# An attention and FFN kernel: FFN chunks that run on over the batches, and the last token tiles stored in four DMAs each

## Chip, cores, metric

The kernel runs on one core of one Trainium2 chip (trn2). The metric is the device time of one execution in microseconds. Beside the times there is one profiled execution of every kernel; its span runs from the first to the last recorded instruction and is about 2 us shorter than the device time. Executions come in two states. In the slower one the start-up takes 2 to 4 us longer; only fast runs are compared below, and times within one trace are counted from the end of the start-up where that matters.

## The reference

Linear attention with a quadratic feature map feeds a two-layer FFN with squared ReLU. The cut reference:

```python
# q, k, v: (4, 4, 1088, 32); S1, S2: (8, 32); w_in: (128, 2048); w_out: (2048, 128)
phi(x) = outer(S1 @ x, S2 @ x)                # 64 features a head
kv  = sum over tokens of phi(k) v ;  z = sum of phi(k)
attn = (phi(q) kv) / (phi(q) z + 1e-6)
x = attn, as 4352 tokens of 4 heads * 32 = 128 features
h = maximum(x @ w_in, 0)
out = (h * h) @ w_out                         # (4352, 128), float32
```

The FFN is most of the work: 4352 columns (tokens) times 16 blocks of 128 hidden features.

## The kernel before

All tokens stand as columns of `xT` (128 features on the partitions). A chunk of n columns runs through 16 blocks. A block is one matmul with w_in (fp32r), a ReLU on ScalarE, a square on ScalarE or VectorE, and one product with w_out in fp32, which appears in the trace as two instructions. By the paces that the prediction reads at three sizes (0.686, 0.820 and 0.953 us at 320, 384 and 448 columns), a block costs 2.083 ns a column and 20 ns beside. In the same trace (before) the starts of its two w_out instructions lie 269, 322 and 375 ns apart, 0.83 ns a column more, which is two fifths of the 2.083. From that I estimate two fifths for each of the two and one fifth, 0.417 ns a column, for the w_in matmul. TensorE's order is static: the w_out product of unit u, then the w_in matmul of unit u + 4. (A unit is one block, or mostly two where a block has 256 columns.) The attention of the next batch is cut into pieces (`kc`, `kvp`, `qc`, `nd`) that are put between the blocks. The chunk lists restart at every batch, so a batch of 1088 tokens has three chunks, 12 in all:

```python
FC = [[(0, 256), (256, 384), (640, 448)]] + [[(0, 384), (384, 384), (768, 320)]] * (B - 2)
FC += [[(0, 448), (448, 384), (832, 256)]]
...
def ffn1(u, i):                                  # w_in
    nc.tensor.matmul(st["pg", u][:, n * i : n * i + n],
                     w_in[:, 128 * (d0 + i) : 128 * (d0 + i) + 128],
                     st[b, "xT"][:, c0 : c0 + n])
...
def ffn2(u, i, xs=None):                         # w_out, the ordinary chunks
    nc.tensor.matmul(po[0][:, 0:n], w, g, start=(d == 0), stop=(d == NB - 1))
```

The last chunk (256 tokens) is token-major: the w_out weights stream and the result is two tiles of 128 tokens x 128 features, `obl`. Each goes out in one DMA, one from ScalarE, one from SyncE:

```python
def store(eng, i):
    eng.dma_start(
        bass.AP(out.tensor, out.offset + (b * S + c0 // 32 + 4 * i) * 128,
                [[128, 4], [G * 128, 32], [1, 128]]),
        ob[i][:, :])

nc.scalar.copy(ob[0][:, :], po[0][:, 0:128])
store(nc.scalar, 0)
nc.vector.tensor_copy(ob[1][:, :], po[1][:, 0:128])
store(nc.sync, 1)
```

## Time and profile before

| | before |
|---|---|
| device time, median of the first runs | 188.1 us |
| span of the profiled run | 186.1 us |
| TensorE busy | 180.4 us (97%) |
| last matmul ends, after the start of the span | 182.21 us |
| end of the last copy to the end of the span | 3.51 us |

The prediction shows the lines that carry the bound. Two groups of the page's costliest instructions are added here:

```profile
L619 PE MATMUL po<-g,w_o 128*128 128x384 f32 (+3 forms) x352 | 138.4, 478 | 0.0
L581 PE MATMUL pg<-xT,w_in 128*128 128x384 f32 (+3 forms) x192 | 110.2, 582 | 0.5 <-ACT gt L590 0.5
```

```profile
L1069 ACTq DRAIN  x2: 8/246/485, 182.3 to 185.6; - x2
```

The last column of the groups says that TensorE hardly ever stood idle before an FFN matmul (0.5 us in all): whatever is gained there must come from the matmuls' own pace.

### The profile page before, as it was taken

The numbers are of one execution on the slowest core, as the hardware profiler recorded it, in microseconds if no ns is written. First come the engines' busy times: TensorE is split into PE (matmuls) and PEld (weight loads), VectorE is DVE, ScalarE is ACT, GpSimd is POOL, SyncE is SP. The second block draws the span as 40 slices with busy tenths as digits, with TensorE's granted clock in tenths as the row PEclk, the third lists the DMA queues.
The fourth block names the chain that finished last, engine by engine and source line by source line (L and its number), as shares of the span: only waits on it lengthen the run. The fifth ranks groups of instructions, "written<-read, shape, count | busy, mean of one in ns | idle before, by whom it ended". The sixth has DMA issues, their size and how long they took to land.

```text
span 186.1 us, 4132 instructions
## 1 busy us (share of the span) xinstructions
PE 180.4 (97%) x1561; PEld 120.8 (65%) x1562; DVE 116.7 (63%) x263; ACT 149.3 (80%) x329; POOL 35.8 (19%) x157
## 2 busy tenths in 40 slices
PE   8998999999999999999999999999999999999991
PEld 2766766666555566666577666656577655666891
DVE  4979989958991699379934689379943412222400
ACT  3509778878979889789698989789698998999960
POOL 2736405327400000184000000185000000000000
PEclk9999999999999999999999999999999999999999
DMA  5899600100039600200059200200020200020200
GB/s 181 201 301 330 168 0 5 28 4 0 4 48 250 153 4 0 45 3 0 13 120 270 38 4 0 42 4 0 8 40 0 35 0 2 8 41 4 30 12 28
DMA packets 24555, 11.27 MB, mean 61 GB/s; under 512 B 17880, under 2 KB 23000, under 8 KB 24536
## 3 DMA queue, kind: packets, MB, share of 16 engines
q1 hardware_dynamic: 24084, 10.82, 24.5%
q8 instruction: 12, 0.20, 0.5%
q10 hardware_dynamic: 452, 0.20, 0.4%
q14 instruction: 7, 0.06, 0.1%
HBM read 8.78 MB, written 2.23 MB: 59 GB/s over the span
## 4 chain that ended last, share of the span: by engine, by line
PE 95%; DMA 2%; DVE 1%; ACT 0%; issue 0%; POOL 0%; ACTq 0%; DVEq 0%
PE po L619 60%; PE pg L581 18%; PE nd L531 3%; PE kvp L397 2%; PE pol L614 2%; PE po L614 2%; PE qc L299 2%; DMA s_nat<-in_S_dram 2%; PE kvp L379 1%; PE kf L309 1%; PE kc L299 1%; PE x L713 1%; ACT gt L590 0%; PE den L774 0%; PE num L774 0%
## 5 line engine op out<-in xcount | busy, mean ns | idle before, releaser
L619 PE MATMUL po<-g,w_o 128*128 128x384 f32 (+3 forms) x352 | 138.4, 478 | 0.0
L581 PE MATMUL pg<-xT,w_in 128*128 128x384 f32 (+3 forms) x192 | 110.2, 582 | 0.5 <-ACT gt L590 0.5
L590 ACT ACTIVATE gt<-pg 128x384 f32<-128x384 f32 (+4 forms) x177 | 85.3, 489 | 19.3 <-PE pg L581 16.1
L619 PEld LDWEIGHTS po<-g,w_o 128*128 128x128 f32 x352 | 62.5, 189 | 22.6 <-issue 7.4
L598 ACT ACTIVATE g<-gt 128x384 f32<-128x384 f32 (+3 forms) x138 | 70.9, 531 | 2.9
L581 PEld LDWEIGHTS pg<-xT,w_in 128*128 128x128 f32 x192 | 36.0, 189 | 25.0 <-issue 6.0
L600 DVE TENSOR_TENSOR g<-gt 128x384 f32<-128x384 f32 (+4 forms) x39 | 21.9, 563 | 38.4 <-ACT gt L590 38.4
L438 POOL COPY kv<-kvt 32x64 f32<-32x64 f32 x48 | 11.8, 246 | 71.3 <-PE po L619 63.0
L492 POOL COPY rd<-rc 32x9 f32<-32x9 f32 (+2 forms) x80 | 16.6, 207 | 13.2 <-DVE rc L484 9.9
L501 DVE STREAM_SHUFFLE qa<-qc 128x576 f32<-128x576 f32 (+2 forms) x20 | 11.6, 648 | 0.0
L516 DVE TENSOR_TENSOR qp<-qa,qb 128x576 f32<-128x576 f32 (+2 forms) x20 | 10.8, 600 | 0.0
L464 DVE STREAM_TRANSPOSE qt<-qc 128x576 f32<-128x576 f32 (+2 forms) x10 | 5.8, 615 | 6.2 <-PE qc L299 6.2
L350 DVE TENSOR_TENSOR kp<-fs 128x576 f32<-128x576 f32 x12 | 8.2, 741 | 0.0
L623 DVE STREAM_TRANSPOSE oT<-po 128x384 f32<-128x384 f32 (+3 forms) x11 | 6.1, 559 | 1.8 <-PE po L619 1.8
L531 PE MATMUL nd<-qp,kv 32*32 32x288 f32 (+2 forms) x320 | 6.8, 353 | 0.0
L341 DVE STREAM_TRANSPOSE fs<-kc 128x576 f32<-128x576 f32 x6 | 4.3, 762 | 3.2 <-PE kc L299 3.2
L550 DVE TENSOR_TENSOR xT<-nd,bc 128x576 fp32r<-128x576 f32 (+2 forms) x10 | 5.6, 600 | 1.0 <-PE nd L531 1.0
L531 PEld LDWEIGHTS nd<-qp,kv 32*32 32x32 f32 x320 | 3.8, 103 | 3.6 <-issue 1.7
L501 DVE STREAM_SHUFFLE qb<-qc 128x576 f32<-128x576 f32 (+2 forms) x10 | 6.0, 646 | 0.0
L541 DVE STREAM_TRANSPOSE bc<-rd 128x576 f32<-128x576 f32 (+2 forms) x10 | 5.8, 606 | 0.2
L292 DVE STREAM_TRANSPOSE qT<-qn 128x192 f32<-128x192 f32 (+3 forms) x11 | 5.8, 564 | 0.0
L614 PE MATMUL pol<-w_o,g 128*128 128x128 f32 x32 | 5.7, 275 | 0.0
(94 smaller groups left out, 94.1 us busy)
## 6 DMA issues: line engine op xcount, KB each, us to landing
kn<-in_k_dram SPq DMA_DIRECT2D x3, 544.0 KB, 6.3
qn<-in_q_dram SPq DMA_DIRECT2D x3, 544.0 KB, 6.7
vn<-in_v_dram SPq DMA_DIRECT2D x9, 144.0 KB, 5.3
out_dram<-oT SPq DMA_DIRECT2D x24, 48.0 KB, 1.8
w_in<-in_moe_w_in_dram SPq DMA_DIRECT2D x4, 256.0 KB, 5.6
w_o<-in_moe_w_out_dram SPq DMA_DIRECT2D x4, 256.0 KB, 6.5
out_dram<-oT SPq DMA_DIRECT2D x8, 56.0 KB, 1.9
vn<-in_v_dram SPq DMA_DIRECT2D x3, 112.0 KB, 6.1
```

What stands on the lines that cost most here:

```text
L350: nc.vector.tensor_tensor(out=_ap(st[b, "kp"], 0, 128, 2 * o, [[64, NT], [8, 8], [1, 8]]), in0=_ap(fs, 0, 128, o, [[32, NT], [1, 8], [0, 8]]),
L438: nc.gpsimd.tensor_copy(_ap(st[b, "kv"], 32 * c, 32, 64 * h, [[32, E], [1, 32]]), _ap(st["kvt"], 32 * h, 32, 0, [[64, E], [1, 32]]),)
L492: nc.gpsimd.tensor_copy(st[b, "rd", i0][32 * h : 32 * h + 32, n * c : n * c + n], st["rc"][32 * c : 32 * c + 32, n * h : n * h + n],)
L501: nc.vector.stream_shuffle(in_=banks(st[b, "qc", i0], 2 * x, 0, m), out=_ap(st[b, which, i0], 0, 128, 2 * m * x, [[m, 2], [1, m]]), mask=m ...
L516: nc.vector.tensor_tensor(out=st[b, "qp", i0, e][:, r], in0=st[b, f"qa{e}", i0][:, r], in1=st[b, "qb", i0][:, r], op=mult,)
L531: nc.tensor.matmul(nd[32 * h : 32 * h + 32, 512 * c : 512 * c + m], kv[r, o : o + 32], qp[r, m * h : m * h + m], start=(e == 0), stop=(e = ...
L581: nc.tensor.matmul(st["pg", u][:, n * i : n * i + n], w_in[:, 128 * (d0 + i) : 128 * (d0 + i) + 128], st[b, "xT"][:, c0 : c0 + n],)
L590: nc.scalar.activation(gt[:, 0:w], st["pg", u][:, 0:w], Relu)
L598: nc.scalar.activation(g2[:, 0:w], gt[:, 0:w], Square)
L600: nc.vector.tensor_tensor(out=g2[:, 0:w], in0=gt[:, 0:w], in1=gt[:, 0:w], op=mult)
L614: nc.tensor.matmul(po[x // 128][:, 0:128], g[:, x : x + 128], w, start=(d == 0), stop=(d == NB - 1),)
L619: nc.tensor.matmul(po[0][:, 0:n], w, g, start=(d == 0), stop=(d == NB - 1))
```

## The change

The intent is to have fewer and wider chunks, hence fewer blocks, and a shorter last transfer. `xT` becomes one tile for all batches, so that a chunk may straddle two batches; there are 10 chunks, five of them 512 wide. A straddling chunk is stored in eight DMAs instead of four. Each of the last two tiles goes out as four DMAs of 32 tokens, alternately from SyncE and ScalarE.

```diff
-    FC = [[(0, 256), (256, 384), (640, 448)]] + [[(0, 384), (384, 384), (768, 320)]] * (B - 2)
-    FC += [[(0, 448), (448, 384), (832, 256)]]
+    FC, at = [], 0
+    for n in (256, 384, 448, 448, 512, 512, 512, 512, 512, 256):
+        FC.append((at, n))
+        at += n
...
+    xT = sb("xT", B * S + SP - S, F32R)
...
-            st[b, "xT"][:, c0 : c0 + n],
+            xT[:, c0 : c0 + n],
...
-    def f_out(b, c0, n):
-        for dm in range(4):
+    def f_out(c0, n):
+        for b in range(B):
+            lo, hi = max(c0, b * S), min(c0 + n, b * S + S)
+            if lo >= hi:
+                continue
+            i0, m = (lo - b * S) // 32, (hi - lo) // 32
+            for dm in range(4):
...
-        def store(eng, i):
-            eng.dma_start(
-                bass.AP(
-                    out.tensor, out.offset + (b * S + c0 // 32 + 4 * i) * 128,
-                    [[128, 4], [G * 128, 32], [1, 128]],
-                ),
-                ob[i][:, :],
-            )
+        def store(i):
+            for x, eng in enumerate((nc.sync, nc.scalar, nc.sync, nc.scalar)):
+                eng.dma_start(
+                    bass.AP(
+                        out.tensor,
+                        out.offset + (b * S + (c0 - b * S) // 32 + 4 * i + x) * 128,
+                        [[G * 128, 32], [1, 128]],
+                    ),
+                    ob[i][32 * x : 32 * x + 32, :],
+                )
```

(The rest of the diff renames indices: chunks no longer carry a batch.)

More of the change, by code (lines that the diff above doesn't have):

```diff
@@ L547, in a_x @@
         m = 8 * nb
-        if (b, "xT") not in st:
-            st[b, "xT"] = bpool.tile([128, SP], F32R, tag="xT", name="xT")
         nc.vector.tensor_tensor(
-            out=_ap(st[b, "xT"], 0, 128, 32 * i0 + 2 * m * x, [[m, k], [1, m]]),
+            out=_ap(xT, 0, 128, S * b + 32 * i0 + 2 * m * x, [[m, k], [1, m]]),
             in0=banks(st[b, "nd", i0], 2 * x, 0, m, k),
@@ L558 @@
     units, first_unit, dur = [], {}, []
-    for b in range(B):
-        for ci, (c0, n) in enumerate(FC[b]):
-            first_unit[b, c0] = len(units)
-            nb = 512 // n
-            sizes = [nb] * (NB // nb)
-            if (b, ci) == (0, 0):
-                sizes = [1, 1] + [2] * 7
-            d0 = 0
-            for m in sizes:
-                units.append((b, ci, c0, n, d0, m))
-                dur.append(m * (5 * n / 2400 + 0.015))
-                d0 += m
+    for ci, (c0, n) in enumerate(FC):
+        first_unit[c0] = len(units)
+        nb = 512 // n
+        sizes = [nb] * (NB // nb)
+        if ci == 0:
+            sizes = [1, 1] + [2] * 7
+        d0 = 0
+        for m in sizes:
+            units.append((ci, c0, n, d0, m))
+            dur.append(m * (5 * n / 2400 + 0.015))
+            d0 += m
     NU = len(units)
-    last = len(FC[B - 1]) - 1
+    last = len(FC) - 1
     g2s = {}
     def ffn1(u, i):
-        b, ci, c0, n, d0, m = units[u]
+        ci, c0, n, d0, m = units[u]
         if i == 0:
@@ L583, in ffn1 @@
             w_in[:, 128 * (d0 + i) : 128 * (d0 + i) + 128],
-            st[b, "xT"][:, c0 : c0 + n],
+            xT[:, c0 : c0 + n],
         )
     def relu(u):
-        w = units[u][3] * units[u][5]
+        w = units[u][2] * units[u][4]
         gt = fpool.tile([128, 512], F32, tag="gt", bufs=GT, name="gt")
@@ L593, in square @@
     def square(u, eng):
-        w = units[u][3] * units[u][5]
+        w = units[u][2] * units[u][4]
         g2 = fpool.tile([128, 512], F32, tag="g2", bufs=G2, name="g2")
@@ L603, in ffn2 @@
     def ffn2(u, i, xs=None):
-        b, ci, c0, n, d0, m = units[u]
+        ci, c0, n, d0, m = units[u]
         d = d0 + i
         if d == 0:
-            st["po", b, c0] = [psf.tile([128, 512], F32, tag="po", name="po")]
-            if (b, ci) == (B - 1, last):
-                st["po", b, c0].append(att("pol"))
-        po = st["po", b, c0]
+            st["po", c0] = [psf.tile([128, 512], F32, tag="po", name="po")]
+            if ci == last:
+                st["po", c0].append(att("pol"))
+        po = st["po", c0]
         g, w = g2s[u][:, n * i : n * i + n], w_o[:, 128 * d : 128 * d + 128]
-        if (b, ci) == (B - 1, last):
+        if ci == last:
             for x in range(0, n, 128) if xs is None else xs:
@@ L619, in ffn2 @@
             nc.tensor.matmul(po[0][:, 0:n], w, g, start=(d == 0), stop=(d == NB - 1))
-    def f_oT(b, c0, n):
-        oT = fpool.tile([128, 448], F32, tag="oT", bufs=2, name="oT")
-        nc.vector.transpose(oT[:, 0:n], st["po", b, c0][0][:, 0:n])
-        st["oT", b, c0] = oT
-    def f_out(b, c0, n):
-        for dm in range(4):
-            nc.sync.dma_start(
-                bass.AP(
-                    out.tensor, out.offset + (b * S + c0 // 32) * 128 + 32 * dm,
-                    [[G * 128, 32], [128, n // 32], [1, 32]],
-                ),
-                _ap(st["oT", b, c0], 32 * dm, 32, 0, [[32, n // 32], [1, 32]]),
-            )
@@ L636, in f_last, with f_oT @@
-    def f_last(b, c0):
-        po = st["po", b, c0]
-        def store(eng, i):
-            eng.dma_start(
-                bass.AP(
-                    out.tensor, out.offset + (b * S + c0 // 32 + 4 * i) * 128,
-                    [[128, 4], [G * 128, 32], [1, 128]],
-                ),
-                ob[i][:, :],
-            )
+    def f_oT(c0, n):
+        oT = fpool.tile([128, 512], F32, tag="oT", bufs=2, name="oT")
+        nc.vector.transpose(oT[:, 0:n], st["po", c0][0][:, 0:n])
+        st["oT", c0] = oT
@@ new lines, in f_out @@
+    def f_out(c0, n):
[5 more added lines that the diff above has]
+            for dm in range(4):
+                nc.sync.dma_start(
+                    bass.AP(
+                        out.tensor, out.offset + (b * S + i0) * 128 + 32 * dm,
+                        [[G * 128, 32], [128, m], [1, 32]],
+                    ),
+                    _ap(st["oT", c0], 32 * dm, 32, lo - c0, [[32, m], [1, 32]]),
+                )
@@ L648, in f_last @@
+    def f_last(c0):
+        po, b = st["po", c0], B - 1
+        def store(i):
+            for x, eng in enumerate((nc.sync, nc.scalar, nc.sync, nc.scalar)):
+                eng.dma_start(
+                    bass.AP(
+                        out.tensor,
+                        out.offset + (b * S + (c0 - b * S) // 32 + 4 * i + x) * 128,
+                        [[G * 128, 32], [1, 128]],
+                    ),
+                    ob[i][32 * x : 32 * x + 32, :],
+                )
         ob = [fpool.tile([128, 128], F32, tag="obl", bufs=2, name="obl") for _ in range(2)]
@@ L649, in f_last @@
         nc.scalar.copy(ob[0][:, :], po[0][:, 0:128])
-        store(nc.scalar, 0)
+        store(0)
         nc.vector.tensor_copy(ob[1][:, :], po[1][:, 0:128])
-        store(nc.sync, 1)
+        store(1)
     def cast_wi(c):
@@ L798 @@
     nc.vector.transpose(bc0[:, :], _ap(rd0, 0, 128, 0, [[1, 8], [0, 32]]))
-    st[0, "xT"] = bpool.tile([128, SP], F32R, tag="xT", name="xT")
     nc.vector.tensor_tensor(
-        out=st[0, "xT"][:, 0:256], in0=num0[:, 0:256], in1=bc0[:, :], op=mult
+        out=xT[:, 0:256], in0=num0[:, 0:256], in1=bc0[:, :], op=mult
     )
@@ L809, with unit_at @@
         t += 1.14 * dur[u]
+    def unit_at(x):
+        return first_unit[max(c for c, _ in FC if c <= x)]
     def due(b, c0):
-        c = max(c for c, _ in FC[b] if c <= c0)
-        return tu[first_unit[b, c]] - LA
+        return tu[unit_at(b * S + c0)] - LA
     def dve(n):
@@ L901, in nd_tasks @@
                 uses=[("bc", b, i0, x), ("nd", b, i0)],
-                rings=[("xT", 2)] if x == 0 and (i0 == 0) else [],
             )
@@ L912, in k_tasks @@
     def k_tasks(b, k0, ks_lead):
-        s0 = tu[first_unit[b - 1, 0]] - 4.0 if b > 1 else 0.0
+        s0 = tu[unit_at(b * S - S)] - 4.0 if b > 1 else 0.0
         O.add(
@@ L985 @@
     for u in range(NU):
-        b, ci, c0, n, d0, m = units[u]
+        ci, c0, n, d0, m = units[u]
         w = n * m
         xt = [
-            ("x", b, i0, x) for i0, k in AC[b] for x in range(2)
-            if 32 * i0 + 16 * k * x < c0 + n and c0 < 32 * i0 + 16 * k * x + 16 * k
+            ("x", b, i0, x) for b in range(B) for i0, k in AC[b] for x in range(2)
+            if b * S + 32 * i0 + 16 * k * x < c0 + n
+            and c0 < b * S + min(32 * i0 + 16 * k * x + 16 * k, S)
         ]
@@ L1023 @@
         pe2.append(mm2s)
-        if d0 + m == NB and (b, ci) != (B - 1, last):
-            po = [x for u_ in range(first_unit[b, c0], u + 1) for x in pe2[u_]]
-            O.add(("oT", b, c0), {"DVE": dve(n)}, tu[u] + 3.0, [], on(f_oT, b, c0, n), uses=po,
+        if d0 + m == NB and ci != last:
+            po = [x for u_ in range(first_unit[c0], u + 1) for x in pe2[u_]]
+            O.add(("oT", c0), {"DVE": dve(n)}, tu[u] + 3.0, [], on(f_oT, c0, n), uses=po,
                   rings=[("oT", 2)])
             O.add(
-                ("out", b, c0), {"SP": 2.0}, tu[u] + 4.0, [], on(f_out, b, c0, n),
-                uses=[("oT", b, c0)],
+                ("out", c0), {"SP": 2.0}, tu[u] + 4.0, [], on(f_out, c0, n),
+                uses=[("oT", c0)],
             )
@@ L1043 @@
     O.run()
-    f_last(B - 1, FC[B - 1][last][0])
+    f_last(FC[last][0])
 _INS = ['q', 'k', 'v', 'S1', 'S2', 'moe_w_in', 'moe_w_out']
```

## The prediction

Part 1's two constants follow from the three paces alone: 0.953 - 0.820 = 0.133 us for 64 columns is 2.083 ns a column, and 0.820 us less 384 of these leaves 20 ns. Part 5's -0.5 is an estimate from the landings and issues of the earlier stores; the 0.05 taken off is the author's estimate, without a number behind it. In the rival about ScalarE, by durations in the trace before, relu and square take 1.001, 1.107 and 1.218 us together at 384, 448 and 512 columns, so 0.106 and 0.111 more, where TensorE's block took 0.133 more. The 1.14 us there is an estimate: where the two alternate, relu starts lie 0.93 us apart at 384 columns and 1.04 to 1.06 at 448.

> **What bounds the kernel now.** I read the page's busy table first, then the chain that ended last, then that chain in order of time, then the last five microseconds.
>
> ```profile
> PE 180.4 (97%) x1561; PEld 120.8 (65%) x1562; DVE 116.7 (63%) x263; ACT 149.3 (80%) x329; POOL 35.8 (19%) x157
> PE 95%; DMA 2%; DVE 1%; ACT 0%; issue 0%; POOL 0%; ACTq 0%; DVEq 0%
> ```
>
> TensorE is busy for 97% of the span and owns 95% of the chain. So nothing counts except what shortens TensorE's own stream or the two ends that lie outside it (about 14 us of set-up, which the change leaves alone, and about 4 us after the last matmul). [...] I measured the pace of the FFN blocks. One block is one w_in matmul (fp32r) and one w_out product (fp32, two instructions). The chain in order of time gives the start of each w_out pair:
>
> ```profile
> 66.13 0.65 PE po L619 x2
> ...
> 75.15 0.65 PE po L619 x2
> ...
> 92.22 0.54 PE po L619 x2
> ...
> 99.77 0.54 PE po L619 x2
> ...
> 145.59 0.75 PE po L619 x2
> ...
> 157.03 0.75 PE po L619 x2
> ```
>
> The first pair of lines spans 11 blocks of 384 columns: 9.02/11 = 0.820 us. The second spans 11 blocks of 320: 7.55/11 = 0.686 us. The third spans 12 blocks of 448: 11.44/12 = 0.953 us. [...] So a block costs 2.083 ns per column plus a constant 20 ns, and there is no bubble left to remove: PE waits for no one in these stretches. The last chunk confirms it. It has five matmul instructions in a block instead of three, and its blocks follow at 0.568 us for 256 columns (0.533 + 0.034). Both constants are near 6.7 ns an instruction.
>
> Then the end:
>
> ```profile
> 181.65 0.66 ACTq L640 DMA_DIRECT2D out_dram<-obl  x1
> 182.25 0.29 DVE L651 COPY obl<-pol 128x128 f32<-128x128 f32 x1 [6.52 <-PE pol L614]
> 182.57 0.69 SPq L640 DMA_DIRECT2D out_dram<-obl  x1
> ```
>
> ```profile
> SPq L1069 <- DMA out_dram<-obl: 1.7, 2, 0.9
> ```
>
> ```profile
> 183.80:184.00 0.20, 0.00 (x0) 0.00 (x0) 0.00 (x0) 0.00 (x0) 0.00 (x0) 1.00 0.13 33
> 184.00:184.20 0.20, 0.00 (x0) 0.00 (x0) 0.00 (x0) 0.00 (x0) 0.00 (x0) 1.00 0.24 61
> 184.20:184.40 0.20, 0.00 (x0) 0.00 (x0) 0.00 (x0) 0.00 (x0) 0.00 (x0) 1.00 0.30 90
> 184.60:184.80 0.20, 0.00 (x0) 0.00 (x0) 0.00 (x0) 0.00 (x0) 0.00 (x0) 1.00 0.23 67
> ```
>
> The last matmul ends at 182.21, the copy at 182.54, and SyncE issues the last store at 182.57. It then waits 1.7 us for the two stores, to about 185.0, and the program's closing barrier takes the rest to 186.1. The windows (the last two numbers are the DMA share and GB/s) show the last store moving from about 183.9 to 184.8 at a share near 0.25[...].
>
> [...]
>
> **The change part by part.**
>
> 1. Fewer, wider chunks. The old lists have 12 chunks, the new list 10, for the same 4352 columns. Every chunk runs through 16 blocks, so 192 blocks become 160. The column cost (4352 x 16 x 2.083 ns = 145 us) does not change. 32 blocks less, at 20 ns each: -0.64 us, all on the chain. The first three chunks (256, 384, 448) and the last one (256, the token-major form) keep their sizes; a 512 block should take 1.0667 + 0.020 = 1.087 us.
>
> 2. ScalarE and VectorE. The instruction order of the changed kernel has 145 units instead of 177, so 32 relus fewer (2 x 0.380 + 16 x 0.481 + 32 x 0.534 + 95 x 0.588 = 81.4 us by the old durations of the sizes, where it was 85.3), 22 squares on VectorE instead of 39, and one oT transpose of 512 (about 0.7 us) per chunk. None is on the chain. Worth zero, if they keep up (below).
>
> 3. xT as one tile over all batches. It removes a ring of two buffers and adds no instruction. The ordered waits show that the w_in matmuls after each attention block wait for ScalarE alone, not for VectorE's later writes to the same tile, so the shared tile adds no false wait. Zero.
>
> 4. Stores of the ordinary chunks. Chunks that straddle a batch take 8 DMAs instead of 4, 48 in all instead of 44, off the path while TensorE runs. Zero.
>
> 5. The last two token tiles. Each becomes four DMAs of 16 KB, two on each queue. [...] I estimate the landing from the earlier stores, which already run on 32 partitions:
>
> ```profile
> out_dram<-oT SPq DMA_DIRECT2D x8, 56.0 KB, 1.9
> out_dram<-oT SPq DMA_DIRECT2D x4, 32.0 KB, 1.7
> ```
>
> 192 packets of 128 B more cost 0.2 us, so 32 packets instead of the 256 of the smaller one should land about 1.5 us after issue. The second store on a queue starts after the first one's issue; that took 0.32 to 0.46 us (shortest and median of the earlier stores), say 0.4. So the last landing is 182.57 + 0.4 + 1.5 = 184.5 instead of 185.0: -0.5 us. I take off 0.05 for six more stores to be waited for. Call it -0.45.
>
> Sum: -0.64 - 0.45 = -1.1 us, so 188.1 becomes 187.0 (-0.6%).
>
> **The rivals.**
>
> Attention comes too late for the chunk that straddles a batch. Chunk 2048 to 2560 starts 128 columns before batch 2, and chunk 3072 to 3584 starts 192 before batch 3, so their data are due 4 to 6 us earlier than before. For: VectorE's chain from the end of qc to the last qp takes about 10.0 us (79.75 to 89.74), and nd starts at 90.35, so the margin is only 0.6 us. Against: the scheduler moved the attention earlier as well. Between qc and nd the new order has ten w_out products and nine or ten w_in matmuls, 10.5 to 10.6 us by part 1's constants, so the margin stays. After nd, six blocks of 1.09 us pass before the first column of batch 2 is read, and VectorE needs about 2 us for it. The tightest place is batch 2's kc to kvp: eight blocks of 448, or 7.6 us, where VectorE's work up to the last ks takes 7.2; but kvp begins with matmuls that need only kp. If one of these slips, it costs 0.2 to 1 us: 187.2 to 188.
>
> ScalarE becomes the bound. With VectorE in attention, ScalarE does relu and square alone. At 512 that takes 0.588 + 0.630 by durations, but starts follow one another more closely: at 448, 0.953 us for both, exactly PE's pace, with no PE bubble. [...] Where relu and its own square alternate, I expect 1.14 us against 1.087, 0.3 to 0.7 us of lag over six to fourteen blocks, inside the lead of four blocks (4.3 us). If it did bind, up to +0.5 us.
>
> The split stores gain nothing. If the time to landing is all fixed latency, or four issues crowd the queues, the -0.45 turns into 0 to +0.3: 187.4 to 187.8. For it: the old store spent about 1.3 us between issue and first packet[...]. Against: the earlier stores land in 1.7 to 1.9 us with eight to fourteen times as many packets.
>
> **Range and chances.** All three rivals are tenths of a microsecond; a gain beyond 1.5 us has no source that I can find. I take 186.4 to 187.7 for 8 in 10. A 2% change would be 3.8 us: only a broken overlap in all three batches would lose that, and nothing could gain it. Faster 0.01, within 0.97, slower 0.02.
>
> **What would show each step right or wrong.** Part 1: 512 blocks at 1.087 us in the chain, the last matmul about 0.6 us earlier, w_out pairs 144 instead of 176. Part 5: DMA share well above 0.25 after the last copy, and about 1.9 us instead of 2.4 from last issue to the end of SyncE's wait. Rivals: a wait of PE for DVE at nd or kvp, PE waiting for ACT at w_in, or gaps in the w_out starts during attention. The prediction is wrong if a 512 block takes more than 1.09 us or if the end after the last copy is not shorter.

## More of the kernel before

ScalarE's second drain, at 185.6 us, takes 8 ns. It is a step of the program's closing barrier, which takes 0.795 us here, from the end of SyncE's last wait for a store to the end of the span.

## The result, and the profile after

| | before | after | difference |
|---|---|---|---|
| device time, median (4 runs each, same rounds) | 188.14 us | 187.68 us | ratio 0.998 (0.9959 to 1.0) |
| span of the profiled run | 186.1 | 185.6 | -0.5 |
| first 384-wide block to last matmul | 154.06 | 153.80 | -0.26 (predicted -0.64) |
| end of last copy to end of span | 3.51 | 3.37 | -0.14 (predicted -0.45) |

Ratios here are the mean time of one kernel's fast runs over the mean of the other's fast runs of the same rounds, so not quite the ratio of the medians quoted, which include slow runs. The interval of the ratio reaches 1.0, so the times alone hardly show a gain. The last two rows of the table are read inside one trace, without the start-up, whose length differs by some tenths from run to run. They are the sharper measure, and both parts gained less than half of what was predicted.

The changed kernel's page: span, TensorE's busy time, and the two groups that were shown of before. The idle time before them is as small as it was, and the instruction counts are those of the prediction (160 blocks; 144 w_out pairs with L620, the rest are the last chunk's):

```profile
span 185.6 us, 3865 instructions
...
PE 180.1 (97%) x1466; PEld 104.9 (57%) x1466; DVE 109.4 (59%) x244; ACT 147.4 (79%) x282; POOL 35.5 (19%) x157
...
L620 PE MATMUL po<-g,w_o 128*128 128x512 f32 (+3 forms) x288 | 133.2, 546 | 0.0
L582 PE MATMUL pg<-xT,w_in 128*128 128x512 f32 (+3 forms) x160 | 104.5, 663 | 0.5 <-ACT gt L591 0.5
```

The chain in order of time (start, us, what) gives the pace of the 512 blocks, in two stretches:

```profile
116.41 0.86 PE po L620 x2
...
125.11 0.86 PE po L620 x2
...
149.79 0.86 PE po L620 x2
...
169.47 0.86 PE po L620 x2
```

The first two lines are 8 blocks apart: 8.70/8 = 1.0875 us. The last two are 18 blocks apart: 19.68/18 = 1.0933 us. The same block, with the same columns and without a wait, has two paces. From the recorded starts, a fast block takes 1.0867 us on average and a slow one 1.0933. The 6.7 ns more lie between the start of the w_in matmul and the start of the next w_out product (630 or 637 ns). Of the 70 undisturbed blocks of 512 in a row, 48 are slow: those from 89 to 102 us (after the `nd` piece of batch 2) and all from 127.8 us on (after that of batch 3).

The tail: windows of 0.2 us (the last two numbers are the DMA share and GB/s), SyncE's closing wait (us in total, times, longest), the last stores' time to landing, and ScalarE's drains (DRAIN, under ACTq in the profile) around the closing barrier (shortest, median, longest in ns; first and last start):

```profile
183.40:183.60 0.20, 0.00 (x0) 0.00 (x0) 0.00 (x0) 0.00 (x0) 0.00 (x0) 1.00 0.01 3
183.60:183.80 0.20, 0.00 (x0) 0.00 (x0) 0.00 (x0) 0.00 (x0) 0.00 (x0) 1.00 0.59 144
183.80:184.00 0.20, 0.00 (x0) 0.00 (x0) 0.00 (x0) 0.00 (x0) 0.00 (x0) 1.00 0.08 18
```

```profile
SPq L1079 <- DMA out_dram<-obl: 1.3, 1, 1.3
```

```profile
out_dram<-obl SPq DMA_DIRECT2D x4, 16.0 KB, 1.5
out_dram<-obl ACTq DMA_DIRECT2D x4, 16.0 KB, 1.6
```

```profile
L1079 ACTq DRAIN  x2: 135/143/151, 183.2 to 185.3; - x2
```

The last packets of the stores are gone by 183.89 us instead of 184.82, in a burst at a share of up to 0.59, and the stores land 1.5 and 1.6 us after issue. That is what the prediction wanted. But ScalarE's second drain now takes 135 ns instead of 8, and it also starts 0.27 us later after ScalarE's event than in kernels with a short drain. The closing barrier takes 0.965 us instead of 0.795. And SyncE, after its long wait has ended 2.14 us after the copy, goes through four more waits that end about 0.07 us apart, at 2.21, 2.28, 2.35 and 2.41 (each wait names two semaphores). Before, the waits ended at 0.81, 0.88, 1.70, 2.66 and 2.72: the second store's landing came second to last.

### The profile page after: what moved, and what is told of

It reads as the page before. It is cut to its first block, busy times and chain, and to the rows that moved or that the text cites. A ratio compares the mean times of both kernels' runs of the same rounds, so it can differ in the third digit from the quotient of the medians.

```text
span 185.6 us, 3865 instructions
## 1 busy us (share of the span) xinstructions
PE 180.1 (97%) x1466; PEld 104.9 (57%) x1466; DVE 109.4 (59%) x244; ACT 147.4 (79%) x282; POOL 35.5 (19%) x157
## 4 chain that ended last, share of the span: by engine, by line
PE 95%; DMA 1%; DVE 1%; ACT 0%; issue 0%; POOL 0%; ACTq 0%; DVEq 0%
PE po L620 60%; PE pg L582 18%; PE nd L535 3%; PE kvp L401 2%; PE pol L615 2%; PE po L615 2%; PE qc L303 2%; DMA s_nat<-in_S_dram 1%; PE kvp L383 1%; PE kf L313 1%; PE kc L303 1%; PE x L722 1%; ACT gt L591 0%; PE warm L671 0%; PE num L783 0%; PE den L783 0%
## 5 line engine op out<-in xcount | busy, mean ns | idle before, releaser
L620 PE MATMUL po<-g,w_o 128*128 128x512 f32 (+3 forms) x288 | 133.2, 546 | 0.0
L582 PE MATMUL pg<-xT,w_in 128*128 128x512 f32 (+3 forms) x160 | 104.5, 663 | 0.5 <-ACT gt L591 0.5
L591 ACT ACTIVATE gt<-pg 128x512 f32<-128x512 f32 (+3 forms) x145 | 80.9, 562 | 21.2 <-PE pg L582 20.5
L599 ACT ACTIVATE g<-gt 128x512 f32<-128x512 f32 (+2 forms) x123 | 72.0, 602 | 2.6
L620 PEld LDWEIGHTS po<-g,w_o 128*128 128x128 f32 x288 | 53.0, 189 | 29.8 <-issue 19.9
L582 PEld LDWEIGHTS pg<-xT,w_in 128*128 128x128 f32 x160 | 30.0, 189 | 31.7 <-issue 15.0
L601 DVE TENSOR_TENSOR g<-gt 128x512 f32<-128x512 f32 (+2 forms) x22 | 14.2, 651 | 41.8 <-ACT gt L591 41.8
L624 DVE STREAM_TRANSPOSE oT<-po 128x512 f32<-128x512 f32 (+3 forms) x9 | 5.9, 652 | 8.1 <-PE po L620 8.1
```

The costliest lines, as they stand in the source:

```text
L582: nc.tensor.matmul(st["pg", u][:, n * i : n * i + n], w_in[:, 128 * (d0 + i) : 128 * (d0 + i) + 128], xT[:, c0 : c0 + n],)
L591: nc.scalar.activation(gt[:, 0:w], st["pg", u][:, 0:w], Relu)
L599: nc.scalar.activation(g2[:, 0:w], gt[:, 0:w], Square)
L601: nc.vector.tensor_tensor(out=g2[:, 0:w], in0=gt[:, 0:w], in1=gt[:, 0:w], op=mult)
```

## The experiments

Two theories stood at the start. Theory A: both mechanisms of the prediction act with the size given there, but each has a side cost that it lacked: a second pace of some 512 blocks, and the closing waits and barrier. Theory B: the gains themselves are smaller, because the extra 6.7 ns belong to a 512 block as such and because the split stores save little. The table collects what the traces show of all kernels. "FFN" is the time from the first 384-wide block (the start of the second w_out product of that width, 28.15 us in the kernel before) to the last matmul, "barrier" from the end of SyncE's last wait for a store to the end of the span, "tail" from the end of the last copy to the end of the span. A block counts as slow from 1.090 us on. The three of e5, e9, e15, e17 and e18 and the one of e16 take just 1.090 us, halfway.

| kernel | FFN | slow 512 blocks of 70 | SyncE's waits end after the copy: first, last | barrier | tail | FFN + tail |
|---|---|---|---|---|---|---|
| before | 154.06 | none of 512 | 0.81, 2.72 | 0.795 | 3.51 | 157.57 |
| changed | 153.80 | 48 | 2.14, 2.41 | 0.965 | 3.37 | 157.17 |
| e1_chunks_only | 153.50 | 8 | 0.82, 2.73 | 0.790 | 3.52 | 157.02 |
| e2_stores_only | 154.06 | none of 512 | 2.14, 2.41 | 0.794 | 3.20 | 157.26 |
| e3_nudge64 | 153.76 | 10 | 2.14, 2.41 | 0.969 | 3.38 | 157.14 |
| e4_dve_fill | 154.28 | 44 | 2.15, 2.42 | 0.964 | 3.38 | 157.66 |
| e5_act_pad | 153.50 | 3 | 2.51, 2.78 | 0.790 | 3.57 | 157.07 |
| e6_rotate | 153.80 | 48 | 1.21, 2.12 | 0.971 | 3.09 | 156.89 |
| e7_after_again | 153.80 | 48 | 2.14, 2.41 | 0.969 | 3.38 | 157.18 |
| e8_eleven | 153.80 | none of 512 | 1.22, 2.10 | 0.790 | 2.89 | 156.69 |
| e9_both | 153.50 | 3 | 1.57, 2.27 | 0.795 | 3.06 | 156.56 |
| e10_eleven_again | 153.81 | none of 512 | 1.21, 2.11 | 0.791 | 2.90 | 156.71 |
| e11_chunks_again | 153.50 | 8 | 0.81, 2.73 | 0.794 | 3.53 | 157.03 |
| e12_nudge72 | 153.74 | 8 | 2.15, 2.42 | 0.974 | 3.39 | 157.13 |
| e13_last64 | 153.65 | 10 | 2.15, 2.42 | 0.975 | 3.39 | 157.04 |
| e14_last72 | 153.65 | 10 | 2.15, 2.42 | 0.974 | 3.40 | 157.05 |
| e15_pad1 | 153.50 | 3 | 2.15, 2.42 | 0.794 | 3.21 | 156.71 |
| e16_pad64 | 153.45 | 1 | 2.15, 2.42 | 0.795 | 3.21 | 156.66 |
| e17_rotate_pad1 | 153.50 | 3 | 1.21, 2.10 | 0.794 | 2.90 | 156.40 |
| e18_pad1_timed | 153.50 | 3 | 2.15, 2.42 | 0.790 | 3.21 | 156.71 |

e7, e12 and e13 have a start-up longer by 3.7, 3.8 and 2.2 us than the changed kernel's. The ratios below are coarser than these intervals: the changed kernel, e7 and e3 agree in FFN + tail within 0.04 us (0.03%), but their ratios are 0.998, 0.9988 and 0.9958.

### The two halves alone

**e1_chunks_only**: the changed kernel with the old stores of the last tiles.

```diff
-        store(0)
+        store(nc.scalar, 0)      # one DMA of 64 KB again
-        store(1)
+        store(nc.sync, 1)
```

> The ten chunks alone, with the old two stores at the end. The profile of the changed kernel puts the last matmul 0.28 us earlier than before (181.93 against 182.21), where 0.64 was predicted; if the two parts add up, this kernel gains about 0.3 us (ratio 0.9985) and its end after the last matmul stays at 3.8 us. If the stores disturb the stream of matmuls, the last matmul comes 0.6 us earlier (181.6). The blocks of 512 should again show two paces, 1.087 and 1.093 us.

Measured: 187.98 us against 188.23, ratio 0.9981 (0.9965 to 0.9997). Only 8 of the 512 blocks are slow, and the FFN gains 0.56 us, near the 0.64 of the prediction. Of the two cases expected it is the one with 0.6 us; 0.3 was thought likelier. The stretch that is slow in the changed kernel is fast here, by the chain of this kernel:

```profile
149.97 0.86 PE po L620 x2
...
168.44 0.86 PE po L620 x2
```

18.47/17 = 1.0865 us. So the slow pace does not belong to a 512 block as such, and Theory B is out for this half.

**e2_stores_only**: the kernel before with the new stores.

```diff
-        store(nc.scalar, 0)
+        store(0)                 # four DMAs of 16 KB, SyncE and ScalarE in turn
-        store(nc.sync, 1)
+        store(1)
```

> The old twelve chunks with the last two token tiles in four stores each. Prediction: 0.45 us. From the profile of the changed kernel: the last landing is 0.5 us sooner after the copy (SyncE's first wait ends 2.1 us after the copy's end instead of 2.6), but four further waits of 0.07 us then follow it instead of one, and the closing barrier took 0.17 us longer. So 0.14 us if the longer barrier belongs to the split stores, 0.3 us if it was chance (ratio 0.9993 or 0.9984).

Measured: 187.79 us against 188.23, ratio 0.9974 (0.9959 to 0.9989). TensorE's part is untouched (154.06). The tail is 0.31 us shorter: the landing comes 0.52 us earlier (2.14 instead of 2.66), and 0.20 us of it go to the waits behind it (2.41 against 2.72 at the end). The barrier has its old length. So the longer barrier of the changed kernel does not come from the split stores alone.

### What sets the pace of a 512 block

**e7_after_again**: the changed kernel without any edit.

> The changed kernel once more, unaltered. Chance theory: the pace of 512-blocks is drawn anew at each restart after a piece of attention, so the pattern (fast to 89.0 us, slow to 102, fast to 127.8, slow to the end) is not repeated exactly, and the number of slow blocks out of 70 differs from 48. Theory of the program: same instructions, same pattern, 48 slow blocks. The barrier at the end is 0.96 us in either case. Ratio expected 0.9965 to 0.998.

**e11_chunks_again**: e1 without any edit.

> The same kernel as e1, one look. If the pace of the 512 blocks is set by the kernel's instructions (as the identical patterns of the changed kernel and its repeat say), 8 slow blocks again, between 102 and 117 us, and 153.50 us of TensorE. If it is set by something of the chip or of one execution, another pattern, and up to 48 slow blocks with 153.80.

e7 gave 187.96 us, ratio 0.9988 (0.9973 to 1.0003); e11 187.8 us, one run. Both repeat their pattern exactly: 48 slow blocks in the same places, and 8. Counted from the first 384-wide block, the starts of all 1113 later TensorE instructions agree to within 3 ns between e1 and e11, and likewise between the changed kernel, e6 and e7, although e7's profile fell in the slow state. So in these runs the pace is not chance and not the state of the chip. It goes with the whole kernel. But it does not go with TensorE's own order alone: e1 and the changed kernel have the same instructions there, differ only in the last stores, and yet have 8 and 48 slow blocks. Their starts agree within 3 ns up to 35.1 us and then part, after a piece of attention; e15's part from the changed kernel's at 29.8 us, although its one extra copy (below) runs only at 135.2. So it is not the work of the edited instructions, which have not run by then. An edit also changes the length of the instruction streams, and e15 adds a small buffer; where programs and buffers lie in memory was not tested.

**e4_dve_fill**: a rival held that VectorE's idleness, or its work, goes with the slow pace. This kernel keeps VectorE busy with an idle multiplication per 512 block (the result of the kernel stays right).

```diff
+    def fill():
+        nc.vector.tensor_tensor(out=scr[:, :], in0=w_in32[:, 0:512], in1=w_in32[:, 0:512], op=mult)
+    ... one fill for each unit of width 512 after the sixth chunk
```

> The changed kernel with useless VectorE products of 128x512 on scratch memory in every idle gap after the last nd, so that VectorE is some 60 to 90% busy until the last chunk. Theory of VectorE: the blocks after 128 us run at 1.087 us instead of 1.093, and the last matmul comes about 0.27 us earlier. Theory of phase: they stay at 1.093 us, or change to one pace at some point without regard to VectorE's share; the time stays within 0.1 us of the changed kernel, if the extra products do not delay squares.

Measured: 188.27 us, ratio 0.9992 (0.9974 to 1.0009). 44 blocks are still slow, with a VectorE that is busy for 35.3 of the 38 us from 128 us on (7.9 in the changed kernel). Three more blocks were held up, by 0.03 to 0.36 us, where TensorE had to wait for VectorE; so its FFN is not to be compared. And in e1 the last stretch is fast with a VectorE that is mostly idle. VectorE is not the cause.

**e3_nudge64**: one extra matmul of 64 columns after each `nd` piece of batches 2 and 3, into a tile that the next matmul overwrites.

```diff
+        if st.pop("nudge", 0):     # set by the nd piece of batch 2 and of batch 3
+            nc.tensor.matmul(st["pg", u][:, 0:64], w_in[:, ...], xT[:, c0 : c0 + 64])
         nc.tensor.matmul(st["pg", u][:, n * i : n * i + n], ...)
```

> The changed kernel with one extra w_in matmul of 64 columns (same values, overwritten at once) right after the attention's nd matmuls of batches 2 and 3. Theory of phase: the pace of a 512-block (1.087 or 1.093 us) is fixed by how TensorE's stream restarts after an inserted piece of attention, so another restart can flip the some 53 blocks that ran at 1.093 to 1.087: last matmul 0.35 us earlier less 0.1 for the two extra matmuls. Theory of VectorE: the pace is 1.087 while VectorE is busy and 1.093 while it idles; then the nudge changes nothing but adds 0.1 us. A third: it is the columns of xT read (those of the straddling chunks); then also nothing.

**e12_nudge72**: the same with 72 columns.

> The changed kernel with one extra 72-column matmul after each nd product of batches 2 and 3 (e3 had 64 columns: the blocks stayed slow after batch 2's and were fast after batch 3's). If the pace depends on where within a grid [...] (6.7 ns, 16 columns) the stream restarts, 72 columns shift it by half a grid against e3, and the pattern after the two nd products changes against e3: fast after batch 2's, or slow after batch 3's. If columns in multiples of 16 or not make no difference, the pattern is that of e3.

e3 gave 187.56 us, ratio 0.9958 (0.9942 to 0.9974), e12 a single 191.3 us with the long start-up. In e3 the stretch after batch 2's `nd` stayed slow and the one after batch 3's became fast. With 72 columns instead of 64 the first one became fast as well, and another stretch (after batch 3's `kc`) became slow. Each extra matmul delays the next w_out product by 103 to 105 ns, which takes back most of what 38 blocks at the fast pace give (38 x 6.7 ns = 0.25 us). From the batch 2 piece on the two kernels differ in eight columns of two matmuls and in nothing else on TensorE, and a stretch of ten blocks changed its pace.

This led to a way of reading the traces. I took the recorded start of every 512 block modulo 6.667 ns (what a slow block takes more than a fast one; by the estimate of 0.417 ns a column for a w_in matmul, it is also the time of 16 columns), averaged it over each stretch, and counted it from the first stretch of the same kernel:

```
kernel           stretch: start us, pace, blocks, phase in ns
changed          79.7 fast 6: 0.0   89.0 slow 10: 2.5   102.0 fast 8: -0.3   116.2 fast 8: -0.4   127.8 slow 38: 2.4
e1_chunks_only   80.0 fast 6: 0.0   89.4 fast 10: 0.0   102.2 slow 8: 2.5    116.6 fast 8: 0.0    128.1 fast 38: 0.0
e3_nudge64       80.0 fast 6: 0.0   89.5 slow 10: 2.3   102.4 fast 8: -0.3   116.7 fast 8: -0.4   128.3 fast 38: -0.4
e12_nudge72      83.6 fast 6: 0.0   93.1 fast 10: -0.2  105.9 slow 8: 2.5    120.3 fast 8: -0.3   131.9 fast 38: -0.4
e15_pad1         79.9 fast 6: 0.0   89.2 fast 1: 4.7    90.3 slow 1: 6.0     91.4 fast 8: 0.1     (and so on)
```

Over the 16 traces with 512 blocks there are 82 stretches of three blocks or more. All 66 fast ones lie between -0.4 and +0.2 ns, all 16 slow ones between 2.3 and 2.8. A stretch that starts at about 4 ns drifts over two blocks, one of them of 1.090 us, and then falls into the fast phase (e5, e9, e15). So TensorE's stream of 512 blocks has two stable phases within a step of 6.7 ns. A fast block takes 163 steps, a slow one 164, so each keeps the phase with which it started after the last attention piece. In the changed kernel the blocks of 384 (820 ns, 123 steps) and 448 (953.3 ns, 143 steps) take whole numbers of these steps too.

**e13_last64** and **e14_last72**: the test of that reading at one place. One extra matmul of 64 or of 72 columns, after batch 3's `nd` only.

```diff
-        st["nudge"] = 64 if b > 1 else 0
+        st["nudge"] = 64 if b > 2 else 0      # and 72 in e14
```

> The changed kernel with one extra 64-column matmul in one place only, after batch 3's nd product (e3 and e12 had it after batch 2's as well). The grid theory, worked out from the traces so far: taken modulo 6.67 ns, all fast stretches of 512 blocks start at one phase (0) and all slow ones 2.4 ns later. 64 columns are 4 whole steps of the grid (16 columns are 6.67 ns), so the last stretch restarts at the phase it has in the changed kernel: it stays slow, 48 slow blocks, and 153.80 plus about 0.03 us from the first 384-wide block to the last matmul. If any extra instruction at that place brings the blocks to the fast pace, 10 slow blocks and 153.58 us.

> The same with 72 columns: 4.5 steps of the grid, which shifts the restart by half a step, from 2.4 to about 5.8 ns. By the grid theory the last stretch is fast, after one or two blocks in between: 10 or 11 slow blocks (those after batch 2's nd product) and 153.58 us. If the theory is wrong and the pace follows from something else, it is the pattern of the run with 64 columns, 153.8 us.

Measured (one run each, 189.65 us with a start-up longer by 2.2 us, and 187.71 us): both have 10 slow blocks. In e14 this is the number expected; in e13 it is not. The chains of e13 (first two lines, 16 blocks) and e14 (16 blocks):

```profile
131.46 0.86 PE po L627 x2
...
148.84 0.86 PE po L627 x2
```

```profile
131.71 0.86 PE po L627 x2
...
149.10 0.86 PE po L627 x2
```

17.38/16 = 1.086 and 17.39/16 = 1.087 us. So 64 columns, by the estimate four whole steps, did not leave the phase as it was. Nor did 72 do anything else: counted from the first 384-wide block, all later TensorE starts of e13 and e14 agree within 1 ns. The matmul after the extra one starts 132 ns after it in both, and the next w_out product comes 103 ns later than in the changed kernel, where the theory had 27 and 30 ns for the columns (estimates, 64 and 72 times 0.417 ns). The eight columns cost nothing here, so e14 came out as expected by luck. That part of the theory, that one can work out the new phase from the columns added, is wrong. What stands is the association without exception: blocks at phase 0 are fast, blocks at phase 2.4 are slow, and the phase is kept until the next attention piece. What a restart's phase follows, beyond being fixed by the kernel, stays open; e3 shows that the same 64 columns keep one restart slow and turn the other fast, and e3 and e12 that 64 and 72 columns part by 2 ns after batch 2's `nd`, enough for the other pace.

### What lengthens the end

**e6_rotate**: Theory: the four waits of 0.07 us come one after the other because SyncE waits first for the semaphore that is completed last. In the changed kernel's trace the DMAs land on eight semaphores. The first closing wait names the one with the latest landing (184.35 us; the last landings of the other seven are at 182.76 to 184.16); in the kernel before, the latest (185.15) is named by the fourth of the five waits. Storing the first chunk in eight DMAs instead of four turns the ring of semaphores, and the last store's is waited for later.

```diff
+            for lo, hi in ((lo, lo + 128), (lo + 128, hi)) if c0 == 0 else ((lo, hi),):
             i0, m = (lo - b * S) // 32, (hi - lo) // 32
```

> The changed kernel with the first chunk's four stores split into eight, far from the end. This turns the ring of eight DMA semaphores by four, so that SyncE's closing waits ask for the last four stores after the four before them and no longer first. Expected: SyncE's five waits, counted from the last copy's end, finish at about 2.28 us instead of 2.41, that is 0.13 us sooner, with the last landing where it was (2.14). If the waits cost only what the landings cost, they still finish at 2.41. In the same profile, which 512-blocks run at 1.093 us is a new throw: if it is chance for every restart, the pattern need not be that of the changed kernel.

Measured: 187.32 us, ratio 0.9963 (0.995 to 0.9975). SyncE's closing waits in this trace (us in total, times, longest):

```profile
SPq L1080 <- DMA out_dram<-obl: 0.9, 2, 0.6
```

The waits end at 1.21, 1.28, 1.93, 2.00 and 2.12: the others pass while the last store is still under way. That is 0.29 us less than in the changed kernel, where 0.13 was expected: all four waits behind the landing are gone. The barrier is still 0.971.

**e5_act_pad**: six tiny ScalarE copies more, in the last full chunk. Their results are not used.

```diff
+    idle = sb("idle", 8)
+    for u in [u for u in range(NU) if units[u][0] == 7][: 2 * 6 : 2]:
+        O.add(("pad", u), {"ACT": 0.2}, ..., emit=on(lambda: nc.scalar.copy(idle[:, :], zero_a[:, :])))
```

> The changed kernel with six useless ScalarE copies of 128x8 in the next-to-last chunk. In the three profiles that hold both parts of the change, ScalarE's drain in the closing barrier came 0.27 us late and the barrier took 0.96 us; with either part alone it took 0.79. Theory of the instruction stream's place: it depends on how many instructions ScalarE has run (some 320 in the late cases, 317 or 386 in the others), so six more bring the barrier back to 0.79 us. Theory of the stores: the four extra issues beside the shorter stream do it, and the barrier stays at 0.96. The copies should cost nothing on the chain.

Measured: 187.44 us, ratio 0.9968 (0.9952 to 0.9984). The barrier is back at 0.790. But the first wait ends at 2.51 instead of 2.14. As a side effect 3 blocks are slow instead of 48 (the FFN takes 153.50 us).

**e9_both**: e5 and e6 together.

> The changed kernel with both mends of the tail: the first chunk's store in eight DMAs (as in e6) and six tiny extra ScalarE copies (as in e5). If the two act separately, SyncE's last wait ends about 2.1 us after the last copy (e6: 2.12) and the closing barrier is 0.79 us (e5), so 2.9 us from copy to end, against 3.37 in the changed kernel. If the extra copies delay the landing, as e5's single profile hinted (first wait 2.51 instead of 2.14), it is 3.1 to 3.3. TensorE from the first 384-wide block to the last matmul: 153.50 us if most 512 blocks run at 1.087 us, as in e5; 153.80 if 48 run at 1.093, as in e6. Ratio to the kernel before 0.994 to 0.9955 in the first case of the tail, 0.9955 to 0.997 in the second.

Measured: 187.04 us, ratio 0.9952 (0.9932 to 0.9971). The barrier is 0.795, but the waits end at 1.57 to 2.27, later than e6's 1.21 to 2.12. So it was no accident of e5: the six copies mend the barrier and delay the landing.

**e15_pad1** and **e16_pad64**: one copy instead of six; and 64, to see whether the drain's place in groups of 64 instructions matters.

```diff
-    ... [: 2 * 6 : 2]
+    ... [: 2 * 1 : 2]                      # e15
+    ... units of chunks 4 to 8, the first 64   # e16
```

> The changed kernel with one tiny extra ScalarE copy in the last full chunk, where e5 had six. If the late drain of ScalarE (closing barrier 0.97 instead of 0.79 us) depends on just how many instructions stand in ScalarE's stream before it, one is enough: barrier 0.79, and the drain takes about 8 ns instead of 135. If the six copies acted through their time or number, the barrier stays at 0.97. The waits end at 2.14 to 2.41 us after the last copy; if they come later, as in e5 (2.51 to 2.78), the extra copies delay the landing. 512 blocks: e5 and e9 had 3 slow ones; 48 if one copy does not reach TensorE's phase.

> The changed kernel with 64 tiny extra ScalarE copies spread over the 512-wide chunks. If the drain is late wherever it falls on the first place of a group of 64 (or 32, or 16) instructions[...], the barrier is 0.97 again, although e5's six copies and e15's one gave 0.79. If the number does not matter in this way, 0.79. The copies take 12 us of ScalarE's 38 idle ones and may make TensorE wait; that is not what the run is for.

Measured (one run each): 187.14 and 186.92 us. One copy is enough, and 64 do as well: barriers of 0.794 and 0.795 us, and no later landing (2.15). So the drain's place in groups of 64 is not what counts. What goes with the longer barrier shows in the DMA view, which lists packets by queue and kind. Here are the changed kernel from 184.5 to 186.5 us, then e15 from 184 to 186.6 us:

```profile
DMA packets 1, 0.01 MB, mean 4 GB/s; under 512 B 0, under 2 KB 0, under 8 KB 0
...
q14 instruction: 1, 0.01, 1.4%
```

```profile
q14 instruction: 1, 0.01, 1.0%
```

and of e5 between 181.4 and 182.8 us:

```profile
q14 instruction: 1, 0.01, 2.7%
```

One packet of 8192 bytes is of the kind `instruction`. By its start in the traces it falls at 186.06 us in the changed kernel, 0.78 us after the start of ScalarE's drain at 185.28. With one ScalarE copy more it falls at 184.27, before the drain at 184.92; with six at 181.86 (e5) and 181.91 (e9); with 64 at 149.3. As more ScalarE copies move it, I take it for part of ScalarE's own stream and call it the refill, though no view names its engine; in all 20 traces the last packet of this kind starts when ScalarE has begun 316 to 321 of its recorded instructions, and in the changed kernel the drain is the 320th of 321. In all eight kernels with a barrier of 0.96 us or more (the changed one, e3, e4, e6, e7, e12, e13, e14) such a packet starts 0.6 to 0.9 us after the start of that drain. In none of the kernels with 0.79 does one start in the 1.5 us after it. The drains of e15:

```profile
L1083 ACTq DRAIN  x2: 8/79/150, 183.1 to 184.9; - x2
```

The last one takes 8 ns again and starts 0.07 us after ScalarE's event instead of 0.35. In the changed kernel the late drain falls into the barrier: GpSimd's event, which counts the engines' drains by a semaphore, comes at 185.45 us, 0.03 after ScalarE's drain has ended (185.42, the last of the drains), and the last events of the other engines follow at 185.57 to 185.58. The barrier is 0.17 us longer. The drain does not wait for the packet's bytes, though: the packet starts after the drain and even after the span's end (185.63). So the traces show the packet's place and the late drain together; what takes the time is not shown. In e5 and e9 the packet falls among the last stores' packets (it takes 0.60 and 0.42 us on its engine), and the landing is later by 0.37 and 0.36 us at the first wait.

### What can be gained

**e8_eleven** and **e10_eleven_again**: eleven chunks without any of 512, since blocks of 384 and 448 had shown one mean pace each so far (0.820 and 0.953 us). e10 is e8 unchanged.

```diff
-    for n in (256, 384, 448, 448, 512, 512, 512, 512, 512, 256):
+    for n in (256, 384, 448, 448, 448, 448, 448, 448, 384, 384, 256):
```

> Eleven chunks that never use 512 columns (256, 384, 448 six times, 384 twice, 256), with the split stores. Blocks of 384 and 448 have shown only one mean pace (0.820 and 0.953 us) in all profiles so far. 16 blocks less than before: 16 x 0.020 = 0.32 us for certain; the ten chunks save 0.64 less what the slow pace takes (0.05 to 0.47 us). So its last matmul should come 0.32 us earlier than before relative to the first 384-block (153.74 us instead of 154.06), with no spread, and its time should be equal to the changed kernel's within 0.2 us.

> The same kernel as e8 (eleven chunks, none of 512 columns), to see whether its result repeats. All its 448 blocks at 0.953 us, 384 at 0.820, none in a second pace: 153.80 us from the first 384-wide block to the last matmul, copy to end 2.89 us, closing barrier 0.79. Ratio 0.995 (0.994 to 0.9965). If e8 was luck of one execution, the tail is back at 3.2 to 3.4 us and the ratio at 0.997.

Measured: 187.23 us, ratio 0.9953 (0.994 to 0.9967), and 187.07 us, ratio 0.9953 (0.9939 to 0.9967). All 448 blocks keep one mean pace; in the chain of e8:

```profile
124.58 0.75 PE po L620 x2
...
143.65 0.75 PE po L620 x2
```

19.07/20 = 0.9535 us. 16 blocks less than before gain 0.26 us where 16 x 20 ns = 0.32 were due. That equals the changed kernel's gain from 32 blocks less. Its time was expected within 0.2 us of the changed kernel's; in the same rounds e7, which is that kernel, took 187.96 us, 0.7 more, of which the tail shows 0.49. The tail is 2.89 and 2.90 us, since it has both mends without being made for them: the waits are in e6's order (1.22 to 2.10), and the barrier is 0.790. Eleven chunks mean other numbers of stores and of ScalarE instructions; which of them did it was not tried. In e8's trace the last packet of instructions (see above) falls at 167.35 us, far from the barrier, which fits.

**e17_rotate_pad1** and **e18_pad1_timed**: the ten chunks with e6's rotation and one ScalarE copy; and e15 again, timed.

> The changed kernel with the first chunk's store in eight DMAs (e6) and one tiny extra ScalarE copy (e15). Theory: [...] an 8 KB packet of the instruction queue that falls on the closing barrier in every kernel with a barrier of 0.97 us, and one instruction more moves it to a place where ScalarE waits anyway (in e15 184.27 us, before the drain). In e5 and e9 six copies moved it further, onto the store issues (181.9 us), and the landing came later (first wait 2.51 and 1.57 us). So here: SyncE's waits end at 2.12 us after the last copy as in e6, barrier 0.79, 2.90 us from copy to end (e9: 3.06). TensorE from the first 384-wide block to the last matmul 153.50 (3 slow 512 blocks, as in e15). Against the kernel before, 157.57 us for both parts, that is 156.40: ratio 0.9938 (0.992 to 0.9955). If the refill is not it, 3.06 or more from copy to end and 0.9952 as in e9.

> The kernel of e15 again, timed: the changed kernel and one tiny ScalarE copy more. From its one trace: TensorE 153.50 us and 3.21 from copy to end, together 156.71 against 157.17 in the changed kernel and 157.57 before. So ratio to before 0.9954 (0.994 to 0.997), where the changed kernel had 0.998; the same traces again, as a kernel's TensorE stream has so far repeated to 3 ns. If e15 was luck, 0.998.

Measured: e17 186.8 us against 188.1, ratio 0.9932 (0.9919 to 0.9946), the shortest of all by FFN and tail; e18 187.32 us, ratio 0.9955 (0.9941 to 0.9969). The FFN and the tail came as expected in both, with 3 slow blocks each. In e17, span, closing wait and drains:

```profile
span 185.1 us, 3872 instructions
```

```profile
SPq L1084 <- DMA out_dram<-obl: 0.9, 2, 0.6
```

```profile
L1084 ACTq DRAIN  x2: 8/82/155, 183.1 to 184.7; - x2
```

e9 and e17 differ only in the number of copies, six and one. Their tails are 3.06 and 2.90 us, with the packet at 181.91 and at 184.31. So the slow blocks, the waits and the longer barrier can all be had back by edits that do no useful work: against before, FFN and tail together gain 1.17 us. That the prediction's sum was 1.1 is in part chance: the two parts gain 0.56 and 0.61, where 0.64 and 0.45 were predicted.

## Why the prediction was right or wrong

The predicted time (187.0 us, range 186.4 to 187.7) holds the measured 187.68 at its edge. The gain was 0.2% where 0.6% was predicted, so as a forecast of the change it was wrong.

- **Part 1, fewer blocks (-0.64).** The mechanism was right: columns cost what they did, 32 blocks went away, and TensorE waits no more than before. The step that failed is "a 512 block should take 1.0667 + 0.020 = 1.087 us". The constant of 20 ns was measured at 320, 384 and 448 and carried to 512, where it is 20 ns in one phase and 26.7 in the other. 48 blocks at 6.7 ns more are 0.32 us. With that, -0.64 + 0.32 = -0.32, and -0.26 was measured. Where few blocks are slow (e1, e11, e15, e18) the gain is 0.56. What is left over after the slow blocks, 0.02 to 0.07 us by kernel, was not looked into. Why this kernel has 48 slow blocks and e1 has 8 stays open.
- **Parts 2 to 4 (zero).** They held: no wait of TensorE for ScalarE beyond the old 0.5 us, none at `nd` or `kvp`.
- **Part 5, the split stores (-0.45).** The size of the gain in the landing was right to 0.02 us: -0.52 where -0.5 was estimated from the earlier stores. In part this is luck, as both ends were put some 0.15 us too early: the old landing is recorded at 185.15 us and was read as 185.0, and the new one came 2.10 us after the copy, where 184.5 means 1.96. The two errors cancel. The DMA share went up to 0.59 in a window of 0.2 us, where the old store kept to 0.23 to 0.30. The step that failed is "I take off 0.05 for six more stores to be waited for": the waits behind the landing take 0.27 us (2.14 to 2.41), where 0.06 followed it before, so 0.20 is lost. e6 shows that the order of the waits costs it: turned, they end at 2.12 instead of 2.41.
- **A term that was missing.** The prediction let the barrier "take the rest" at its old length. It grew by 0.17 us. ScalarE's stream has 321 recorded instructions now instead of 382, and the last refill starts 0.78 us after the start of its drain in the barrier. e15 moves it with one instruction to 0.65 us before that drain, and the barrier is 0.794 again; what takes the time is not shown. -0.52 + 0.20 + 0.17 = -0.15; -0.14 was measured.
- **The rivals.** Attention coming late and ScalarE as the bound did not occur. "The split stores gain nothing" was right in effect by about a third of a microsecond (0.14 gained of 0.45), but for none of the reasons given there.
- **What was named as proof.** "The prediction is wrong if a 512 block takes more than 1.09 us": 48 of 70 did.

## What to carry to other kernels

When a gain is a few tenths of a microsecond, count what stands behind it on the path: here the slowest transfer stood at the head of a list of waits, the four behind it took about 0.07 us each, and with the order turned (e6) the list ended 0.29 us sooner. Compare the closing barrier and the instruction packets of both traces before believing that a shorter tail is a better tail; here one idle instruction moved the refill from 186.06 to 184.27 us, and the barrier went from 0.965 back to 0.794 (e15). And a constant per block fitted at three sizes is not known at a fourth: read the pace in every stretch, since the same block had two here, 1.087 and 1.093 us.
